# Decode attention with a GLU gate: the gate's weights moved to the front of the stream, vector-matrix products on VectorE

## The chip, the cores and the metric

The kernel runs on one core of one Trainium2 chip. A core has five engines that run side by side, each with its own list of instructions: TensorE (PE: matmul, with its weight loads as PEld), VectorE (DVE), ScalarE (ACT), GpSimd (POOL) and SyncE (SP). They meet through semaphores. Sixteen DMA engines move data between the chip's memory (HBM) and the core's own memory (SBUF, 128 partitions); here SP issues nearly all transfers, ACT a few small ones. Matmuls write to PSUM. The metric is the time of one execution in device microseconds, as the median of several runs; the profile is of one more execution, taken by the hardware profiler.

## The reference

One token is decoded. Its row x has 512 values. It is normalised, attends with 32 heads over 8192 cached keys and values of 128 each, and the result is multiplied by a gate that a GLU block computes from the same normalised row.

```python
xn = _layernorm(x, axis=-1)                                   # (1, 1, 512)
# attention: q of 32 heads of 128, caches of (1, 32, 8192, 128)
q = (xn @ wq).reshape(B, Sq, H, Dh).transpose(0, 2, 1, 3)     # wq (512, 4096)
scores = jnp.einsum("bhqd,bhkd->bhqk", q, k_cache) * (Dh ** -0.5)
p = _softmax(scores, axis=-1)
o = jnp.einsum("bhqk,bhkd->bhqd", p, v_cache)
s = o.transpose(0, 2, 1, 3).reshape(B, Sq, H * Dh) @ wo       # wo (4096, 512)
# gate
g = jnp.einsum("bsd,df->bsf", xn, w_gate)                     # (512, 1376)
u = jnp.einsum("bsd,df->bsf", xn, w_up)                       # (512, 1376)
g = _silu(jnp.einsum("bsf,fd->bsd", _sigmoid(g) * u, w_down)) # (1376, 512)
return x + s * g
```

All of it is float32. The caches are 134 MB each, wq and wo 8.4 MB each, the gate's three matrices 2.8 MB each: 293.7 MB are read once.

## The kernel before, in words

The 32 heads are taken in 16 pairs. The keys of a pair (8.39 MB) fill one *slot*: 128 partitions of 64 KB. Partitions 0 to 63 hold the first head, 64 to 127 the second, and each partition holds 128 consecutive positions of 128 values. There are three slots: `slots[0]` and `slots[1]` take the keys in turn, `slots[2]` takes the values, and before them wq.

**The queries.** wq is loaded first (`ld_wq`), then the keys of pairs 0 and 1. x comes on ACT's queue, once as a column over the partitions (`x_col`) and once as four rows (`x_row`, for the end). VectorE, TensorE and ACT compute mean and variance; `xn` is the normalised column. TensorE multiplies xn with wq: 32 matmuls with one column of xn as weights (L206), whose results lie in single rows of PSUM. ACT copies these rows (L211), TensorE spreads each over all partitions with a column of ones (L218), and ACT copies the heads to their halves of `q_all` (L225).

**One pair.** VectorE multiplies the keys in place by the query (`scores`, L281), sums each position (L282) and takes the partition's maximum (L284). TensorE transposes the maxima (L246), VectorE takes each head's maximum (L276), TensorE spreads it (L248), and ACT turns the scores into powers (`powers_of`, L294 and L296). TensorE multiplies powers and values in 32 matmuls (L255, the function `pair`) into `po`, ACT copies `po` (`parts`, L301), four small matmuls add up its pieces (L260), and VectorE divides by the sum of the powers (`heads_out`, L288 and L289). The two heads are then rows of a small tile `on`, and two DMAs on ACT's queue put them into `o_all` in the layout that the last product wants (`place`).

**What sets the order.** Everything is written out by hand. Each engine runs its list in order, and every step counts up its engine's semaphore. TensorE's 15 first pairs are a loop of its own (L265) around the same block; the last pair is written out behind it. SP issues the loads: the keys of pair i when the scores of pair i - 2 are summed, the values of pair i - 1 when the values of pair i - 2 have been used. Whatever SP has issued waits in its DMA queue, in order.

**The end.** The last values go into the slot of keys 14 (L331). Behind them come the gate's weights w_gate, w_up and w_down, into `slots[2]` as soon as values 14 are used, and then wo in six pieces of 14, 10, 4, 2, 1 and 1 rows per partition (`W_ENDS`), into the slot of keys 15. After the last pair TensorE computes the gate's two products with xn (L356), ACT and VectorE form `sg` and `hg`, VectorE transposes them in blocks (L366), TensorE multiplies with w_down (L384), and ACT and VectorE finish the gate in `g_row`. Then come wo's matmuls (L402 and L406; the results of the first 28 rows per partition are copied by ACT and folded in, L371 and L377), two VectorE operations (L416 and L418) and the output.

## Time and profile before

| what | us |
|---|---|
| median of 3 runs (lowest, highest) | 687.7 (687.37, 688.03) |
| profiled execution: its span | 685.6 |
| VectorE busy in it | 574.0 (84%) |
| TensorE busy in it | 222.1 (32%) |
| ACT busy in it | 40.9 (6%) |
| granted TensorE clock, mean | 0.664 of full speed |
| idle time of VectorE before the keys' products (L281), waiting for keys | 38.8 |

The span goes from the profiled execution's first instruction to its last; no other time is shown for that execution, so its own time is the span, and the runs' median stands 2.1 us above it. Busy shares say how long an engine had work, not that it set the end. Rows of groups read: line, engine, operation, output<-input with shapes, count | busy us, mean ns of one | idle us before it and what ended the idle time. Rows of the timeline read: start, duration, engine, line, operation, with the idle time before it and its releaser in brackets. Rows of waits read: who <- whom: total us, times, longest.

### The profile page before, as it was taken

Reading aid. Unit: us, or ns where it says so; the run is one execution under the profiler, and the core shown is the slowest. Engines: PE = TensorE matmul, PEld = TensorE weight load, DVE = VectorE, ACT = ScalarE, POOL = GpSimd, SP = SyncE. Lnnn points to the kernel's source line nnn. Section 1 sums busy time; section 2 is a strip of 40 time slices with the busy share of each in tenths; the row PEclk is TensorE's granted clock in tenths of the full one; section 3 lists DMA queues with packets and bytes.
Section 4 is the critical chain, followed back from the end, with each engine's and each line's share of the span. In section 5 each row is a group of like instructions: output and inputs, shape, how many; then the busy total and the mean of one; then the engine's idle time right before and its main releaser. Section 6 shows DMA issues by size and latency. Waiting matters only on the chain.

```text
span 685.6 us, 3694 instructions
## 1 busy us (share of the span) xinstructions
PE 222.1 (32%) x1570; PEld 62.7 (9%) x1570; DVE 574.0 (84%) x136; ACT 40.9 (6%) x122; POOL 0.7 (0%) x6
## 2 busy tenths in 40 slices
PE   0550230605041140505042140506042140605656
PEld 0110000101010010101001010101000010101121
DVE  0159999999999999989898989989898989989220
ACT  0040100000000000000001010000001010000010
POOL 0000000000000000000000000000000000000000
PEclk9965575757566575757557575756657575756798
DMA  9999999999999999999999999999999999999996
GB/s 375 440 445 451 428 428 428 432 428 428 428 436 444 448 440 428 428 428 436 428 428 428 440 444 451 428 432 428 432 432 428 428 440 436 451 436 428 405 434 285
DMA packets 6614, 293.84 MB, mean 429 GB/s; under 512 B 1096, under 2 KB 1104, under 8 KB 1616
## 3 DMA queue, kind: packets, MB, share of 16 engines
q1 hardware_dynamic: 6200, 293.74, 99.1%
q10 hardware_dynamic: 408, 0.02, 0.0%
q8 instruction: 4, 0.07, 0.0%
q14 instruction: 2, 0.02, 0.0%
HBM read 293.74 MB, written 0.00 MB: 428 GB/s over the span
## 4 chain that ended last, share of the span: by engine, by line
DMA 37%; DVE 30%; PE 0%; SPq 0%; issue 0%
DMA slot<-in_A_k_cache_dram 31%; DVE slot L281 15%; DVE sc L282 15%; DMA slot<-in_A_wo_dram 6%; PE acc L406 0%; SPq L131 0%; PE pt L246 0%; PE acc L377 0%; DVE g_row L416 0%; DVE g_row L418 0%; DVE mx L276 0%
## 5 line engine op out<-in xcount | busy, mean ns | idle before, releaser
L281 DVE TENSOR_TENSOR slot<-slot,q_all 128x16384 f32<-128x16384 f32 x16 | 275.5, 17217 | 38.8 <-DMA slot<-in_A_k_cache_dram 38.8
L282 DVE TENSOR_REDUCE sc<-slot 128x128 f32<-128x16384 f32 x16 | 275.5, 17220 | 0.6
L255 PE MATMUL po<-slot,weights 128*8 128x512 f32 x1024 | 146.7, 737 | 232.1 <-PEq L242 231.5
L255 PEld LDWEIGHTS po<-slot,weights 128*8 128x8 f32 x1024 | 30.3, 103 | 335.3 <-issue 334.6
L246 PE MATMUL pt<-ident,mx 128*1 128x128 f32 x32 | 8.8, 374 | 148.6 <-PEq L242 148.6
L301 ACT COPY o<-po 128x512 f32<-128x512 f32 x16 | 9.4, 586 | 385.2 <-PE po L255 385.2
L260 PE MATMUL pn<-o,pick 128*2 128x128 f32 x128 | 16.5, 272 | 12.8 <-PEq L242 12.8
L180 DVE TENSOR_REDUCE st<-x_col 128x1 f32<-128x4 f32 x1 | 0.2, 157 | 20.7 <-DMA x_col<-in_A_x_dram 20.7
L246 PEld LDWEIGHTS pt<-ident,mx 128*1 128x1 f32 x32 | 1.8, 80 | 154.1 <-issue 154.1
L288 DVE RECIPROCAL rl<-pn 2x1 f32<-2x1 f32 x16 | 2.3, 146 | 14.6 <-PE pn L260 14.6
L294 ACT ACTIVATE nb<-pm 128x2 f32<-128x2 f32 x16 | 2.8, 173 | 190.4 <-PE pm L248 190.4
L416 DVE TENSOR_TENSOR g_row<-g_row,acc 128x128 f32<-128x128 f32 x1 | 0.3, 289 | 15.3 <-PE acc L406 15.3
L296 ACT ACTIVATE weights<-sc,nb 64x128 f32<-64x128 f32 x32 | 12.8, 399 | 0.9
L260 PEld LDWEIGHTS pn<-o,pick 128*2 128x2 f32 x128 | 9.9, 84 | 29.6 <-issue 27.2
L248 PE MATMUL pm<-mx,ones 1*128 1x2 f32 x32 | 8.8, 344 | 7.4 <-PEq L242 7.4
L402 PE MATMUL big<-slot,o_all 128*1 128x512 f32 x56 | 9.4, 765 | 4.8 <-DMA slot<-in_A_wo_dram 4.8
L250 PE MATMUL pn<-rs,half 128*2 128x1 f32 x32 | 3.0, 163 | 23.5 <-PEq L242 23.5
L218 PE MATMUL big<-q_all,ones 1*128 1x512 f32 x16 | 8.8, 850 | 1.6 <-ACT q_all L225 0.8
L206 PE MATMUL big<-slot,xn 128*1 128x512 f32 x64 | 9.0, 726 | 0.8 <-DVE xn L198 0.8
L248 PEld LDWEIGHTS pm<-mx,ones 1*128 1x128 f32 x32 | 7.9, 306 | 14.4 <-issue 14.4
L276 DVE TENSOR_REDUCE mx<-pt 1x2 f32<-1x128 f32 x16 | 4.5, 278 | 5.2 <-PE pt L246 5.0
L182 PE MATMUL pt<-st,ones 128*128 128x1 f32 x2 | 0.6, 362 | 23.4 <-DVE st L180 23.4
(61 smaller groups left out, 62.1 us busy)
## 6 DMA issues: line engine op xcount, KB each, us to landing
slot<-in_A_wo_dram SPq DMA_DIRECT2D x1, 3584.0 KB, 32.5
slot<-in_B_w_gate_dram SPq DMA_DIRECT2D x1, 2752.0 KB, 16.8
slot<-in_B_w_up_dram SPq DMA_DIRECT2D x1, 2752.0 KB, 22.8
slot<-in_B_w_down_dram SPq DMA_DIRECT2D x1, 2560.0 KB, 27.3
slot<-in_A_wo_dram SPq DMA_DIRECT2D x1, 2560.0 KB, 38.2
slot<-in_A_wo_dram SPq DMA_DIRECT2D x1, 1024.0 KB, 40.2
o_all<-on ACTq DMA_DIRECT2D x32, 0.5 KB
slot<-in_A_wo_dram SPq DMA_DIRECT2D x1, 512.0 KB, 40.9
```

Source lines behind the costliest of these rows:

```text
L206: ins = PE.matmul(big[b][g * GP:g * GP + 1, :], xn[:, k:k + 1], wq_t[:, k, c:c + QT], start=(k == 0), stop=(k == KT - 1))
L218: spreads[t] = pe(PE.matmul(big[t % 2], ones[g * GP:g * GP + 1, :], q_row[g * GP:g * GP + 1, b, :], start=True, stop=True))
L246: PE.matmul(pt[0:1, :], mx[:, 0:1], ident, start=True, stop=True).then_inc(turned, 1)
L248: PE.matmul(pm, ones[:1, :], mx[:1, 1:3], start=True, stop=True).then_inc(spread_m, 1)
L255: ins = PE.matmul(po[g * GP:g * GP + 2 * HT, :], weights[:, j // HT, :], v[:, j * Dh:(j + HT) * Dh], start=(j < HT * NG), stop=(j >= NB - ...
L260: ins = PE.matmul(pn[:, :Dh], pick[:, b:2 * HT:HT], o1[:, b * Dh:(b + 1) * Dh], start=(b == 0), stop=(b == HT - 1))
L276: DVE.reduce_max(mx[:1, 1:3], pt[0:1, :].rearrange("o (e p) -> o e p", e=2), axis=AX.X).then_inc(reduced, 1)
L281: wait(DVE, dve(DVE.tensor_mul(k, k, qb[:, i:i + 1, :].to_broadcast([P, NB, Dh]))))
L282: summed[i] = dve(DVE.reduce_sum(sc[i % 2], k, axis=AX.X))
L296: ACT.activation(weights[h, :, e * HT:(e + 1) * HT], sc[i % 2][h].rearrange("p (g b) -> p g b", b=HT), AF.Exp, bias=nb[h, e:e + 1], scale= ...
L301: ACT.copy(o1, po).then_inc(copied, 1)
L402: ins = PE.matmul(big[0][g:g + 1, :], o_all[:, r:r + 1], wo_t[:, r, :], start=(r < NG), stop=(r + NG >= W_FOLD))
```

## The change

1. **Order of loads.** wq is loaded in two halves, and w_gate and w_up come right behind it, into `slots[0]`; then keys 0, into `slots[1]`. w_down follows into `slots[2]` once the queries are summed, keys 1 into `slots[0]` once the gate's first products are summed, values 0 into `slots[2]` once the gate is summed. Keys use the slots the other way round. Of w_down's last rows only the missing 96 are loaded, not 128. At the end the last keys and the last values are loaded in halves, and wo follows the values directly.
2. **Products on VectorE.** wq, w_gate and w_up are multiplied by xn in place on VectorE: one pass with a product (`tensor_scalar`), then three with product and sum (`scalar_tensor_tensor`). TensorE only adds up the partitions with a block of ones, which for the queries also spreads them. The 32 matmuls L206, ACT's copies L211 and the gate's 56 matmuls L356 go.
3. **x.** Only the four rows are loaded; VectorE transposes them into the column.
4. **Heads.** VectorE transposes each pair's heads into a PSUM tile `o_t`, and after the last pair four transposes put them all into `o_all`. ACT's 32 small DMAs go.
5. **TensorE's text.** TensorE's instructions are noted first (`Later`) and written out at the end: a loop of two turns, whose first turn skips the work and only jumps over it. The whole body is a block with a branch back at its end that is never taken; ACT, VectorE and TensorE carry a branch hint for it, TensorE's in front of the last pair.

SP's list from the start of the program to the first issue that waits for scores. Before:

```order
L131 DMA slot<-in_A_wq_dram 128x16384
L131 DMA slot<-in_A_k_cache_dram 128x16384 x2
L161 DMA slot<-in_A_v_cache_dram 128x16384 [waits s_pe]
L131 UNCONDITIONAL_BRANCH
L131 DMA slot<-in_A_k_cache_dram 128x16384 [waits s_dve]
```

Now:

```order
L163 DMA slot<-in_A_wq_dram 128x8192 x2
L163 DMA slot<-in_B_w_gate_dram 128x5504
L163 DMA slot<-in_B_w_up_dram 128x5504
L163 DMA slot<-in_A_k_cache_dram 128x16384
L212 UNCONDITIONAL_BRANCH
L163 DMA slot<-in_B_w_down_dram 128x5120 [waits s_pe]
L163 DMA slot<-in_B_w_down_dram 96x512
L163 DMA slot<-in_A_k_cache_dram 128x16384 [waits s_pe]
L205 DMA slot<-in_A_v_cache_dram 128x16384 [waits s_pe]
L163 DMA slot<-in_A_k_cache_dram 128x16384 [waits s_dve]
```

Four loads now stand ahead of keys 0, and w_down, keys 1 and values 0 each wait for TensorE (s_pe), where keys 1 waited for nothing.

VectorE's list between the normalisation and the first scores. Before:

```order
L198 TENSOR_SCALAR xn<-xc,st 128x4 [waits s_dve]
L228 MEMSET acc 128x128
L229 MEMSET po 128x512
L230 MEMSET weights 128x256
L231 MEMSET half 128x2
L234 MEMSET half 64x1 [waits s_dve,s_pool]
L234 MEMSET half 64x1
L236 COPY pick<-ident 32x8 x4
L131 UNCONDITIONAL_BRANCH
L281 TENSOR_TENSOR slot<-slot,q_all 128x16384 [waits s_act,s_k0]
```

Now (s_wq0 and s_wq2 are wq's halves, s_wg and s_wu the gate's matrices):

```order
L260 TENSOR_SCALAR xn<-xc,st 128x4 [waits s_dve]
L266 TENSOR_SCALAR slot<-slot,xn 128x4096 [waits s_wq0,s_dve]
L267 SCALAR_TENSOR_TENSOR slot<-slot,xn 128x4096 [waits s_dve,s_wq0]
L267 SCALAR_TENSOR_TENSOR slot<-slot,xn 128x4096 [waits s_dve,s_wq2]
L267 SCALAR_TENSOR_TENSOR slot<-slot,xn 128x512 [waits s_dve]
L267 SCALAR_TENSOR_TENSOR slot<-slot,xn 128x512 x7
L266 TENSOR_SCALAR slot<-slot,xn 128x1376 [waits s_wg]
L267 SCALAR_TENSOR_TENSOR slot<-slot,xn 128x1376 [waits s_dve] x3
L266 TENSOR_SCALAR slot<-slot,xn 128x1376 [waits s_wu,s_dve]
L267 SCALAR_TENSOR_TENSOR slot<-slot,xn 128x1376 [waits s_dve] x3
L315 MEMSET big 128x512 [waits s_pe,s_act,s_dve]
L316 TENSOR_TENSOR slot<-slot,big 128x352
```

Nineteen passes over weights stand ahead of the first scores, the gate's behind the queries'.

SP's list from the last values on. Before:

```order
L331 DMA slot<-in_A_v_cache_dram 128x16384 [waits s_dve]
L131 DMA slot<-in_B_w_gate_dram 128x5504 [waits s_valued]
L131 DMA slot<-in_B_w_up_dram 128x5504
L131 DMA slot<-in_B_w_down_dram 128x5120
L131 DMA q_all<-in_B_w_down_dram 128x512
L131 DMA slot<-in_A_wo_dram 128x7168 [waits s_dve]
```

Now:

```order
L430 DMA slot<-in_A_v_cache_dram 128x8192 [waits s_dve]
L430 DMA slot<-in_A_v_cache_dram 128x8192
L163 DMA slot<-in_A_wo_dram 128x7168 [waits s_dve]
L163 DMA slot<-in_A_wo_dram 128x5120
L163 DMA slot<-in_A_wo_dram 128x2048
```

The gate's four loads no longer stand between the last values and wo.

The diff, cut to its core:

```diff
-    ld_wq = load(SP, "wq", wq_t, wq.rearrange("(p k) c -> p k c", k=KT))
+    wq_v = wq.rearrange("(p k) c -> p k c", k=KT)
+    ld_wq = [load(SP, f"wq{n}", wq_t[:, n:n + 2, :], wq_v[:, n:n + 2, :]) for n in (0, 2)]
+    wg_t, wu_t = (slots[0][:, n * KT * F:(n + 1) * KT * F].rearrange("p (k f) -> p k f", f=F) for n in range(2))
+    ld_g = load(SP, "wg", wg_t, w_gate.rearrange("(p k) f -> p k f", k=KT))
+    ld_u = load(SP, "wu", wu_t, w_up.rearrange("(p k) f -> p k f", k=KT))
...
     load_keys(0)
-    load_keys(1)
-    ld_x = load(ACT, "x", x_col, xv.rearrange("(p k) -> p k", k=KT))
+    once = nc.alloc_registers("once")
+    nc.regs_mov(once, 0)
+    nc.br("body")
+    body = ctx.enter_context(ExitStack())
+    body.enter_context(nc.body("body"))
+    hints = {e: e.mark_branch_hint_location() for e in (ACT, DVE)}
...
+    def in_place(w, k, cols=slice(None)):
+        y = w[:, 0, cols]
+        if k == 0:
+            return dve(DVE.tensor_scalar(y, y, xn[:, 0:1], None, op0=ALU.mult))
+        return dve(DVE.scalar_tensor_tensor(y, w[:, k, cols], xn[:, k:k + 1], y, op0=ALU.mult, op1=ALU.add))
...
+    for t in range(NQ):
+        c = slice(t * QT, (t + 1) * QT)
+        wait(PE, in_place(wq_t, KT - 1, c), copies.get(t - 2))
+        spreads[t] = pe(PE.matmul(big[t % 2], ones, wq_t[:, 0, c], start=True, stop=True))
...
+    load(SP, "wd", wd_t, w_down[:FP * P, :].rearrange("(p r) e -> p r e", r=FP), spreads[NQ - 1])
+    ld_d = load(SP, "wd", wd_last[:FL, :], w_down[F - FL:, :])
...
+    load_keys(1, rows[1])
...
+    gated = column_sums(big[1], s_gate)
+    load_values(0, gated)
...
     def heads_out(i):
...
-        outs[i] = dve(DVE.tensor_scalar(on[i % 2][:2], pn[:, :Dh], rl[:2], None, op0=ALU.mult))
+        wait(DVE, dve(DVE.tensor_scalar(on[:2], pn[:, :Dh], rl[:2], None, op0=ALU.mult)))
+        o = o_t[:WR, 2 * WP * i:2 * WP * i + Dh].rearrange("r (e a) -> r a e", a=WP)
+        turned_out[i] = dve(DVE.transpose(o, on[:WR].rearrange("e (a r) -> e a r", r=WR)))
...
+    with nc.Fori(0, 2, engines=pe_only) as visit:
+        with PE.engine.If(visit > 0):
+            PE.play(before)
+            with nc.Fori(0, NP - 1, engines=pe_only):
+                PE.play(each)
+    hints[PE.engine] = PE.engine.mark_branch_hint_location()
+    PE.play(last)
+    PE.play(after)
...
+    nc.regs_alu(once, once, 1, op=ALU.add)
+    for e in (ACT, DVE, PE.engine, POOL, SP):
+        br = e.br_lt(once, 1, on_true="body", on_false="done")
+        if e in hints:
+            br.branch_hint(hints[e])
```

In the new text `before` is TensorE's work up to the first pair, `each` one pair of the loop, `last` the last pair and `after` wo's matmuls.

## The prediction

> **What bounds the kernel now.** I read the page's first three parts first, then the chain of work that ended last, then the waits, and last the two ends of the run as a timeline and in narrow windows.

> ```profile
> span 685.6 us, 3694 instructions
> ...
> DMA  9999999999999999999999999999999999999996
> ...
> q1 hardware_dynamic: 6200, 293.74, 99.1%
> q10 hardware_dynamic: 408, 0.02, 0.0%
> q8 instruction: 4, 0.07, 0.0%
> q14 instruction: 2, 0.02, 0.0%
> HBM read 293.74 MB, written 0.00 MB: 428 GB/s over the span
> ```

> The DMA line is 9 in every slice but the last, and SP's queue (q1) alone holds the sixteen DMA engines for 99.1% of the span. The chain names VectorE for 30%, which can mislead; its pieces in order of time say why:

> ```profile
> 526.40 17.24 DVE slot L281
> ...
> 560.91 42.81 DMA slot<-in_A_k_cache_dram
> ...
> 603.74 17.24 DVE slot L281
> ...
> 639.57 40.94 DMA slot<-in_A_wo_dram
> ...
> 681.82 0.44 PE acc L406 x8
> 682.26 0.02 issue
> 682.28 0.30 DVE g_row L416
> ...
> 682.61 0.29 DVE g_row L418
> ```

> VectorE starts a keys' product only when the keys land. Between 526.40 and 603.74 four tiles of 8.39 MB passed: 19.34 us each, 434 GB/s. Keys land 42.8 us after their issue, though one tile takes 19.3: each transfer stands behind a whole one already queued. So the queue is never empty, and VectorE's work only decides when the next issue comes, not when its bytes do. At 434 GB/s, 293.74 MB take 677 us; with some 2 us until the first bytes and 3.9 us after the last landing (681.8, the last matmuls' start, to 685.6) hardly 3 us are left to gain anywhere.

> Where those 3 us lie, windows at the end show (columns: stretch, its length, busy time of the engines, TensorE's granted clock, DMA share, GB/s):

> ```profile
> 670.00:675.00 5.00, 4.09 (x20) 0.73 (x24) 0.00 (x0) 0.00 (x0) 0.00 (x0) 0.50 0.99 426
> ...
> 679.00:680.00 1.00, 1.00 (x12) 0.19 (x8) 0.00 (x0) 0.00 (x0) 0.00 (x0) 1.00 0.96 377
> 680.00:681.00 1.00, 0.93 (x22) 0.31 (x16) 0.00 (x0) 0.48 (x1) 0.00 (x0) 1.00 0.38 145
> 681.00:682.00 1.00, 0.96 (x32) 0.42 (x24) 0.00 (x0) 0.10 (x1) 0.00 (x0) 1.00 0.13 43
> ```

> The mean DMA engine stops at 680 + 0.38 + 0.13 = 680.5, the last landing comes at 681.8: the sixteen end unevenly, and that costs 1.3 us.

> **The change, part by part.** *The stream's order and length.* Since the sum of bytes decides, moving the gate's 8.2 MB from the end to the start is worth nothing by itself. The bytes fall by 32 rows of 2 KB (64 KB, 0.15 us at 428 GB/s). Halving wq, the last keys and the last values gives shorter rows; the wo pieces, with rows still shorter, moved 426 GB/s from 670 to 675 (row above), so I cost it at nothing, with 0.3 us as the other end.

> *Is the queue still fed at the start?* This is the cover for all that VectorE now does, and it has to be counted out.

> ```profile
> 0.96 0.39 SPq L131 DMA_DIRECT2D slot<-in_A_wq_dram  x1
> 23.14 0.16 DVE L180 TENSOR_REDUCE st<-x_col 128x1 f32<-128x4 f32 x1 [20.65 <-DMA x_col<-in_A_x_dram]
> 25.97 0.23 DVE L198 TENSOR_SCALAR xn<-xc,st 128x4 f32<-128x4 f32 x1
> ...
> slot<-in_A_wq_dram SPq DMA_DIRECT2D x1, 22.0
> x_col<-in_A_x_dram ACTq DMA_DIRECT2D x1, 2.0 KB, 22.1
> ...
> L281 DVE TENSOR_TENSOR slot<-slot,q_all 128x16384 f32<-128x16384 f32 x16 | 275.5, 17217 | 38.8 <-DMA slot<-in_A_k_cache_dram 38.8
> L218 PE MATMUL big<-q_all,ones 1*128 1x512 f32 x16 | 8.8, 850 | 1.6 <-ACT q_all L225 0.8
> L225 ACT COPY q_all<-big 64x256 f32<-64x256 f32 x16 | 5.9, 367 | 5.5 <-PE big L218 5.2
> ```

> From wq's landing at 0.96 + 22.0 = 23.0 and 19.34 us per 8.39 MB, the new queue lands wg (2.82 MB, 6.5 us) at 29.5, wu at 36.0, keys 0 at 55.3, wd at 61.8, keys 1 at 81.1, values 0 at 100.5. The same row of VectorE gives 1.051 ns per element. Half of wq lands at 23.0 - 9.7 = 13.3. x was 22.1 us on the way in 128 pieces, 8 for each engine, 2.8 us a turn between wq's pieces; as four pieces it needs one or two turns, say 6 us, and its mean and variance took 3.1 us (23.14 to 26.20). So x is ready at 13.3; if it were not, the end lies 15 us of slack away. The passes over wq: two of 4096 (4.3 us each) to 21.9, the third after 23.0 to 27.3, the last in eight pieces of 0.6 to 32.1. TensorE's sum (0.85) and ACT's two copies (0.73) beside each piece keep near that pace, so the eighth sum is done by 34. Then wd can be issued, 21 us before keys 0 end. The gate's eight passes of 1376 (1.45 us) are done at 43.7, since they follow the queries' passes, and TensorE's sums at 45: keys 1 are issued 16 us before the queue would run dry at 60.8 (1 us from an issue to first bytes). Values 0 wait for the gate's last sum:

> ```profile
> 662.46 2.31 PE L384 MATMUL big<-slot,o 128*1 128x512 f32 x18 [2.68 <-DVE o L367]
> 666.37 0.28 ACT L390 ACTIVATE g_row<-big 128x128 f32<-128x128 f32 x1 [0.52 <-PE big L377]
> ```

> that stretch took 3.9 us before, so 61.8 + 4 = 66, or 70 at half the clock, against 80. Keys 2 wait for the first scores, 55.3 + 34.5 = 89.8 against 99.5. All are fed; the work taken from TensorE and ACT was beside the stream too. Cost: 0.

> *Each pair.* A stream transpose is added on VectorE and two small DMAs of the ACT queue go. VectorE waits 38.8 us over ten products (row above), some 3 us a pair late in the run; a transpose is 0.2 us (row below). Cost: 0.

> *The end.* wo now follows the last values directly, so what follows the values has 19.3 us of wo as cover instead of that and the gate's 19.5.

> ```profile
> 642.44 9.84 PE L255 MATMUL po<-slot,weights 128*8 128x512 f32 x64 [0.57 <-DMA slot<-in_A_v_cache_dram]
> 652.35 0.59 ACT L301 COPY o<-po 128x512 f32<-128x512 f32 x1 [10.82 <-PE po L255]
> 654.34 0.34 DVE L289 TENSOR_SCALAR on<-pn,rl 2x128 f32<-2x128 f32 x1
> 670.91 5.81 PE L402 MATMUL big<-slot,o_all 128*1 128x512 f32 x28 [4.61 <-DMA slot<-in_A_wo_dram]
> 676.87 3.60 PE L402 MATMUL big<-slot,o_all 128*1 128x512 f32 x28 [0.15 <-DMA slot<-in_A_wo_dram]
> ...
> L366 DVE STREAM_TRANSPOSE o<-q_all 128x32 f32<-128x32 f32 x10 | 1.3, 197 | 0.0
> ...
> 660.00:665.00 5.00, 2.54 (x22) 0.54 (x22) 2.26 (x13) 0.00 (x0) 0.00 (x0) 1.00 1.09 461
> 665.00:670.00 5.00, 0.60 (x11) 0.10 (x8) 0.77 (x2) 0.86 (x2) 0.00 (x0) 0.86 0.96 413
> ```

> Let E be the last landing. The second half of the values lands at E - 19.3; half its matmuls, 32, take 4.1 us at full clock (3.60 / 28 each) or 6.6 at half (5.81 / 28). From there to the scaled heads it took 652.28 to 654.68, 2.4 us, and five transposes add 1.2: the heads stand placed at E - 11.6 or E - 9.1. wo's first 14 rows land at E - 10.8. At full clock TensorE then follows the landings. At half clock throughout the first 14 rows end at E - 3.3, the next ten (full clock by then, 2.6) at E - 0.7, four more at E + 0.3, copy and fold at E + 1.3: 1.2 us late. The clock was 1.00 after the 2.7 us gap before L384 and 0.50 (670 to 675, row further up) after the 4.6 us gap before L402; the gaps here are about 2.7, nearest the first. Cost: 0, other end +1.2.

> *Unevenness.* The code and small packets fall on single DMA engines: the four code packets of q8 (16 KB each, 0.6 us at one engine's sixteenth of 428 GB/s), which I take for TensorE's, the longest text, two more of q14, and 408 packets of the ACT queue. The new program has 165 matmuls in TensorE's text instead of 239, no x_col, no head placements; its early visit fetches once more. Bounds: all 1.3 us gained, or 0.6 lost if one more packet falls on the last engine. No view says which engine a packet takes; I take half the gain, -0.6.

> Sum: 685.6 - 0.15 - 0.6 = 684.9 for the profiled execution. The runs' median stands 2.1 us above its span, which I carry over: **687.0 us**, for this case 686.3 to 688.3.

> **The rivals.** *All evenness gained (faster).* If no code packet falls in the stream, E moves to the mean engine's 680.5, less 0.15, and the vanished small packets another 0.1: 686.1 us. For it speaks the shorter text, against it that the two ends of TensorE's code still have to come.

> *TensorE meets missing code at the end (slower).* The program now loops twice over blocks and jumps. If the block behind the last pair is not there when TensorE reaches wo, its fetch queues behind the stream: one turn was 2.8 us for x_col. After the landing of wo's second piece, at E - 4.8, TensorE has no such slack, so it shows in full from there: 687.0 + 2.8 = 689.8. Against it: in the trace of before no matmul group at the end waits for code. [...]

> *The two-tensor product runs at half speed (slower).* Then 3 x 4096 + 6 x 1376 = 20544 elements cost 21.6 us more: the queries' passes end at 43.9, the gate's at 64.1, keys 1 are issued at 65.1 against 60.8, and the queue is empty for 4.3 us: 691.3. It decides as soon as the passes grow by 16 us; if the one-tensor passes run at double speed, 3.6 us come back. The row that is nearest, L281, reads two f32 tensors at 1.051 ns, the same as the one-tensor sum, and speaks against it. [...]

> **How the numbers follow.** 0.2% of 687.7, 1.4 us, is about what a measurement of this kernel tells from no change. Chances: forecast 0.55, evenness 0.17, missing code 0.15, half speed 0.13. Faster is the second case, 0.17. Slower is the third, most of the fourth (0.10) and the cold clock's tail of the first (0.02): 0.27. The rest, 0.56, is the same. The range goes from just under the second case, 685.9, to 690.0, just over the third; it leaves out most of the fourth and the tails, under 0.2.

> **What would show it.** Right: DMA 9 from the first slice to the last; no wait of keys 1 or values 0 beyond their turn; the product passes at 4.3 and 1.45 us; wo's matmuls waiting for wo's landings; the last landing at 681.1, with a steeper fall of the DMA share. Wrong: passes of 8.6 us and a dip in the DMA line near 60 us; an idle TensorE inside wo's rows with all landed; more q8 packets than four.

## The result and the profile after

The changed kernel takes 690.04 us (median of five, 689.67 to 691.09), the kernel before, run beside it, 687.37 us (687.30 to 688.03). The ratio is 1.0038, with a 95% interval of 1.0027 to 1.0049: 2.6 us slower. The forecast was 687.0, no change. One execution of the run e3 below (765.71 us) fell into a slower state of the chip, and the ratios leave it out.

The span did not grow. These are the top and the DMA part of the page of the changed kernel:

```profile
span 685.7 us, 3402 instructions
...
DMA  8999999999999999999999999999999999999996
...
q1 hardware_dynamic: 6600, 293.67, 99.1%
q8 instruction: 2, 0.03, 0.0%
q10 hardware_dynamic: 8, 0.00, 0.0%
HBM read 293.67 MB, written 0.00 MB: 428 GB/s over the span
```

685.7 us against 685.6, the same 428 GB/s, the same 99.1% of the DMA engines' time for SP's queue. The small packets of ACT's queue (q10) have gone from 408 to 8, and q8 has two code packets inside the span instead of four. The end of the chain of waits, in order of time (start, duration, what):

```profile
657.68 24.18 DMA slot<-in_A_wo_dram
681.91 0.44 PE acc L37 x8
682.38 0.30 DVE g_row L471
682.70 0.29 DVE g_row L473
```

The last landing comes at 681.9, as before, and what follows it is what followed it before. (L37 is the line that plays TensorE's noted instructions; it stands for all of them.) Narrow windows of the changed kernel, the last of them behind the span (stretch, its length, busy time of the engines, TensorE's clock, DMA share, GB/s):

```profile
679.00:680.00 1.00, 1.00 (x12) 0.19 (x8) 0.00 (x0) 0.00 (x0) 0.00 (x0) 1.00 0.91 352
680.00:681.00 1.00, 0.93 (x22) 0.31 (x16) 0.00 (x0) 0.43 (x1) 0.00 (x0) 1.00 0.07 27
681.00:682.00 1.00, 0.92 (x28) 0.41 (x24) 0.00 (x0) 0.16 (x1) 0.00 (x0) 1.00 0.03 12
685.70:690.00 4.30, 0.00 (x0) 0.00 (x0) 0.00 (x0) 0.00 (x0) 0.00 (x0) 0.50 0.01 2
```

And the window behind the span of the kernel before:

```profile
685.60:690.00 4.40, 0.00 (x0) 0.00 (x0) 0.00 (x0) 0.00 (x0) 0.00 (x0) 0.78 0.00 0
```

Two things are to be read. First, the profiled execution took 690.04 us, 4.3 us more than its span, and the four others stand 4.2 to 5.5 us above theirs. The kernel before was timed 96 times beside the experiments, each time with its own span: it stands 1.7 to 1.9 us above it, 1.8 in the middle. (The 2.1 us named ahead of the change is the median of three runs less the span of one execution, and is 0.3 us too much.) So some 2.5 of the 2.7 us between the medians lie behind the last instruction that the span counts. There the DMA engines did nothing before (share 0.00, 0 GB/s) and do something now (0.01, 2 GB/s). The packets of the trace say what: one code packet of 16 KB on q8 at 685.05 us, which begins 0.6 us ahead of the span's end and ends behind it, and one of 8 KB on q14 at 687.71. A stretch with no busy engine is shown by no group, wait or chain of the profile; only the windows and the difference between time and span give it away. Second, the mean DMA engine now stops at 680 + 0.07 + 0.03 = 680.1, earlier than before (680.5), but the last one still at 681.9.

### The profile page after: what moved, and what is told of

The parts are those of the page before. It is cut to its first block, busy times and chain, and to the rows that moved or that the text cites. A ratio compares the mean times of both kernels' runs of the same rounds, so it can differ in the third digit from the quotient of the medians.

```text
span 685.7 us, 3402 instructions
## 1 busy us (share of the span) xinstructions
PE 211.8 (31%) x1422; PEld 74.8 (11%) x1422; DVE 606.2 (88%) x166; ACT 39.9 (6%) x120; POOL 0.7 (0%) x6
## 3 DMA queue, kind: packets, MB, share of 16 engines
q1 hardware_dynamic: 6600, 293.67, 99.1%
## 4 chain that ended last, share of the span: by engine, by line
DVE 51%; DMA 35%; SPq 0%; issue 0%; PE 0%
DMA slot<-in_A_k_cache_dram 31%; DVE sc L381 25%; DVE slot L380 25%; DMA slot<-in_A_wo_dram 4%; SPq L163 0%; DVE on L388 0%; DVE o_t L390 0%; DVE mx L372 0%; DVE mx L383 0%; PE pt L37 0%; PE acc L37 0%; DVE g_row L471 0%; DVE g_row L473 0%; DVE rl L387 0%; DVE g_row L417 0%
## 5 line engine op out<-in xcount | busy, mean ns | idle before, releaser
L380 DVE TENSOR_TENSOR slot<-slot,q_all 128x16384 f32<-128x16384 f32 (+1 forms) x17 | 275.6, 16214 | 34.0 <-DMA slot<-in_A_k_cache_dram 34.0
L381 DVE TENSOR_REDUCE sc<-slot 128x128 f32<-128x16384 f32 (+1 forms) x17 | 275.7, 16216 | 0.6
L37 PE MATMUL po<-slot,weights 128*8 128x512 f32 x1024 | 146.8, 729 | 263.9 <-PEq L37 263.9
L37 PEld LDWEIGHTS po<-slot,weights 128*8 128x8 f32 x1024 | 45.5, 102 | 351.9 <-issue 345.1
L37 PE MATMUL pt<-ident,mx 128*1 128x128 f32 x32 | 8.6, 367 | 107.8 <-PEq L37 107.8
L402 ACT COPY o<-po 128x512 f32<-128x512 f32 x16 | 9.4, 587 | 416.9 <-PE po L37 416.9
L267 DVE SCALAR_TENSOR_TENSOR slot<-slot,xn 128x512 f32<-128x512 f32 (+2 forms) x16 | 24.3, 1554 | 3.0 <-DMA slot<-in_A_wq_dram 2.7
L37 PE MATMUL pn<-o,pick 128*2 128x128 f32 x128 | 16.5, 272 | 12.8 <-PEq L37 12.8
L37 PE MATMUL big<-slot,ones 128*128 128x512 f32 (+3 forms) x52 | 12.2, 496 | 25.5 <-DVE slot L267 23.6
L37 PEld LDWEIGHTS pt<-ident,mx 128*1 128x1 f32 x32 | 1.8, 80 | 112.0 <-issue 112.0
L37 PEld LDWEIGHTS pn<-o,pick 128*2 128x2 f32 x128 | 9.9, 84 | 29.5 <-issue 27.1
L37 PE MATMUL pm<-mx,ones 1*128 1x2 f32 x32 | 8.6, 337 | 7.8 <-PEq L37 7.8
L37 PE MATMUL pn<-rs,half 128*2 128x1 f32 x32 | 3.0, 163 | 23.7 <-PEq L37 23.7
L37 PE MATMUL big<-slot,o_all 128*1 128x512 f32 x56 | 8.9, 725 | 2.8 <-DMA slot<-in_A_wo_dram 2.8
L37 PE MATMUL big<-slot,o 128*1 128x512 f32 (+1 forms) x22 | 4.5, 934 | 16.3 <-DMA slot<-in_B_w_down_dram 16.3
L37 PEld LDWEIGHTS pm<-mx,ones 1*128 1x128 f32 x32 | 7.7, 298 | 14.6 <-issue 14.6
L37 PEld LDWEIGHTS big<-slot,ones 128*1 128x1 f32 (+1 forms) x52 | 4.0, 133 | 34.2 <-DVE slot L267 28.3
L283 ACT COPY q_all<-big 64x256 f32<-64x256 f32 x16 | 5.9, 368 | 23.1 <-PE big L37 22.6
```

The lines of the kernel that those rows point to most:

```text
L37: ins = getattr(self.engine, name)(*args, **kwargs)
L267: return dve(DVE.scalar_tensor_tensor(y, w[:, k, cols], xn[:, k:k + 1], y, op0=ALU.mult, op1=ALU.add))
L283: copies[t] = act(ACT.copy(qb[h, 2 * t:2 * t + 2, :], q[h, :, e, :]))
L380: wait(DVE, dve(DVE.tensor_mul(k[:, j, :], k[:, j, :], qb[:, i:i + 1, :].to_broadcast([P, n, Dh]))))
L381: summed[i] = dve(DVE.reduce_sum(sc[i % 2][:, j], k[:, j, :], axis=AX.X))
L402: ACT.copy(o1, po).then_inc(copied, 1)
```

## The experiments

Each run was timed beside the kernel before, whose median was 687.46, 687.57, 687.40 and 687.56 us in the four groups of runs (e1 to e4, e5 to e8, e9 to e12, e13 to e16). A hint here is the pair of calls `mark_branch_hint_location` and `branch_hint`, which ties a place in an engine's list to the branch at the end of the body; that branch is never taken. The length of VectorE's list counts all its instructions in the compiled program, jumps included. Times are medians; the code packets are those of the one profiled execution, by their start; in these traces one of q8 has 16 KB, one of q14 8 KB.

| run | hints on | VectorE's list, instructions | us | ratio (95%) | code packets on q8; q14, us |
|---|---|---|---|---|---|
| changed kernel | ACT, VectorE, TensorE | 200 | 690.04 | 1.0038 (1.0027 to 1.0049) | 6.7, 685.1; 687.7 |
| e1 | none | 199 | 687.58 | 1.0003 (0.9994 to 1.0012) | 6.5, 665.9; 60.5, 170.0 |
| e2 | ACT, TensorE | 199 | 690.11 | 1.0033 (1.0021 to 1.0045) | 6.3, 687.1; 59.9, 687.6 |
| e3 (no visit) | all | 196 | 689.96 | 1.0036 (1.0023 to 1.0049) | 105.0, 688.0; 687.9 |
| e4 (no visit, no branch) | none | 190 | 687.60 | 1.0002 (0.9993 to 1.0010) | 107.5, 667.1; 59.5, 192.1 |
| e5 (kernel before) | ACT, VectorE | 191 | 687.55 | 1.0000 (0.9991 to 1.0009) | 48.9, 647.7, 661.0, 682.4; none |
| e6 | TensorE | 199 | 689.88 | 1.0035 (1.0022 to 1.0048) | 6.6, 688.0; 60.6, 170.2, 687.9 |
| e7 | ACT, VectorE | 200 | 689.80 | 1.0033 (1.0022 to 1.0045) | 6.4, 665.7; 687.5 |
| e8 (visit ahead of the stream) | TensorE | 199 | 690.69 | 1.0035 (1.0021 to 1.0048) | 2.4, 687.7; 60.8, 168.4, 688.1 |
| e9 | ACT | 199 | 687.51 | 1.0000 (0.9991 to 1.0009) | 6.5, 665.9; 60.7, 687.9 |
| e10 | VectorE | 200 | 690.39 | 1.0039 (1.0025 to 1.0053) | 6.4, 665.7; 170.0, 687.5, 690.1 |
| e11 (list shortened) | ACT, VectorE | 190 | 687.51 | 1.0001 (0.9992 to 1.0010) | 6.4, 665.9; none |
| e12 (kernel before, list longer) | ACT, VectorE | 206 | 688.87 | 1.0020 (1.0011 to 1.0029) | 49.3, 647.4, 661.4, 681.7; 683.9, 686.3 |
| e13 | TensorE, late | 199 | 687.60 | 1.0002 (0.9993 to 1.0011) | 6.6, 666.8; 60.6, 170.0 |
| e14 | VectorE, late | 200 | 687.67 | 1.0001 (0.9992 to 1.0010) | 6.4, 665.8; 60.7, 170.0, 687.8 |
| e15 (kernel before, list longer) | ACT, VectorE | 200 | 689.75 | 1.0034 (1.0022 to 1.0046) | 51.5, 647.1, 660.0, 681.4; 686.6, 689.1 |
| e16 | all, late | 200 | 687.62 | 1.0006 (0.9997 to 1.0015) | 6.7, 666.8; 60.7, 170.0 |

### Which part of the change costs the time

The first theory was that the hints, and not the moved work, put missing code behind the end. Rivals were the early visit of TensorE's blocks, the branch and jump, and the new way of placing heads. e1 takes away the hints and nothing else:

```
-    hints = {e: e.mark_branch_hint_location() for e in (ACT, DVE)}
+    hints = {}
...
-    hints[PE.engine] = PE.engine.mark_branch_hint_location()
```

> The changed kernel without any branch hint; the never-taken branch and the two-turn loop stay. Theory A (the 2.7 us lie behind the last instruction: the hints keep the code that follows from being fetched ahead, so it is fetched on demand after the span): time 687.4, about 1.8 us above the span, and the page's queue list shows instruction packets of q14 inside the span again. Rival B (the branch and the extra block at the end cost the time, whatever the hints): 690.0, still 4.3 above the span.

687.58 us: all of the loss is gone. Behind the span of e1:

```profile
685.70:690.00 4.30, 0.00 (x0) 0.00 (x0) 0.00 (x0) 0.00 (x0) 0.00 (x0) 0.77 0.00 0
```

The DMA engines are idle there again. e2 takes the hint from VectorE alone:

```
-    hints = {e: e.mark_branch_hint_location() for e in (ACT, DVE)}
+    hints = {e: e.mark_branch_hint_location() for e in (ACT,)}
```

> The changed kernel without VectorE's hint alone; ACT's and TensorE's stay. Theory A1 (it is VectorE's code that is missing at the end; its text is the longer of the two that fetch by q14): 687.4, one q14 packet inside the span. Theory A2 (TensorE's or ACT's code is what is missing): 690.0. Rival B: 690.0.

690.11 us, where theory A1 had 687.4: VectorE's hint isn't needed for the loss. The loss isn't the same each time: of the six executions of e2 the fastest took 688.00 us. e3 leaves the hints and takes the loop of two turns away, so that TensorE's code is met for the first time when it is needed:

```
-    with nc.Fori(0, 2, engines=pe_only) as visit:
-        with PE.engine.If(visit > 0):
-            PE.play(before)
-            with nc.Fori(0, NP - 1, engines=pe_only):
-                PE.play(each)
+    PE.play(before)
+    with nc.Fori(0, NP - 1, engines=pe_only):
+        PE.play(each)
```

> The changed kernel without the loop of two turns around TensorE's blocks; hints and branch stay. Theory C (one DMA engine ends 1.4 us after the others because the early visit fetches a code packet at 6.7 us): the code packet comes later or not at all, the last landing comes by up to 1.4 us earlier unless a later packet falls on a late engine: span 684.3 to 685.7. Rival D (the late engine comes from the first loads themselves): span 685.7, unchanged. On the time behind the span theory A says 4.3 us as before, 688.6 to 690.0 in all; if the visit were the cause of it, 687.4 or less.

689.96 us: the visit has no part in the loss. Its trace tells something else, on the unevenness. Of the sixteen completions of each load, the first and the last of wq's first half were 1.9 us apart in the changed kernel, 15 of them within 0.4 us; and to the end one completion stays that late (1.8 us at the last wo piece). The only code packet so early is that of TensorE at 6.67 us. Without the visit they lie within 0.41 us, and those of the load that landed last ahead of the packet at 105 us within 0.36; those of the next load are 1.92 us apart, and without the late one 0.34. So one code packet into the running stream made one DMA engine late, and in this run the stream didn't give the time back: the last wo piece's completions are still 1.91 us apart. The theory's landing 1.4 us earlier didn't come, because the later packet did the same as the early one. The windows at the end of e3:

```profile
679.00:680.00 1.00, 1.00 (x12) 0.19 (x8) 0.00 (x0) 0.00 (x0) 0.00 (x0) 1.00 0.81 309
680.00:681.00 1.00, 0.94 (x22) 0.31 (x16) 0.00 (x0) 0.44 (x1) 0.00 (x0) 1.00 0.06 25
681.00:682.00 1.00, 0.91 (x28) 0.41 (x24) 0.00 (x0) 0.14 (x1) 0.00 (x0) 1.00 0.03 12
```

One engine alone fills the last two windows (a sixteenth is 0.06), with or without the visit. e4 leaves out the hints, the branch and the visit:

```
-    once = nc.alloc_registers("once")
...
-    hints = {e: e.mark_branch_hint_location() for e in (ACT, DVE)}
...
-        br = e.br_lt(once, 1, on_true="body", on_false="done")
```

> The changed kernel with neither hints nor the never-taken branch nor the loop of two turns: the moved gate, VectorE's products and the transposes alone. Theory A: 1.8 us above its span, which is 684.3 to 685.7 after theory C and 685.7 after rival D: 686.1 to 687.5. If the cost were in the moved work itself (neither A nor B): 690.

687.60 us. What is left of the change, the moved gate, the products on VectorE, the transposes and the halved loads, is worth nothing either way: 1.0002 (0.9993 to 1.0010).

### Do hints cost by themselves?

If any hint costs, then the kernel before must lose with one too. e5 puts the branch and the hints on ACT and VectorE into it; e6 and e7 split the hints of the changed kernel between TensorE and the other two.

```
     (e5, in the kernel before)
+    once = nc.alloc_registers("once")
+    nc.regs_mov(once, 0)
+    nc.br("body")
...
+    hints = {e: e.mark_branch_hint_location() for e in (ACT, DVE)}
...
+    for e in (ACT, DVE, PE, POOL, SP):
+        br = e.br_lt(once, 1, on_true="body", on_false="done")
+        if e in hints:
+            br.branch_hint(hints[e])
```

> The kernel before, unchanged in its work, with one part of the change alone: the never-taken branch at the end and a hint for it on ACT and VectorE. Theory A (these hints keep the code behind the end from being fetched ahead): the two q14 packets vanish from the span, at least one comes after it, and the time is 690.0, 2.5 above the kernel before with a span of 685.6. Rival E (the cost belongs to the new arrangement of work, which the hints only uncover): 687.4.

A miss: 687.55 us, no loss. Both q14 packets of the kernel before (193.7 and 225.5 us) are gone, and none comes behind the end. So the hints did act, and it cost nothing (687.55 against 687.57 us).

```
     (e6)
-    hints = {e: e.mark_branch_hint_location() for e in (ACT, DVE)}
+    hints = {}
     (e7)
-    hints[PE.engine] = PE.engine.mark_branch_hint_location()
```

> The changed kernel with TensorE's hint alone. Theory A with ACT or VectorE as the culprit (their packets came at 687.6 and 687.7 in the runs that cost time): q14 packets inside the span, one q8 packet behind it, 687.4. If TensorE's packet behind the end costs as much: 690.0.

> The changed kernel with the hints of ACT and VectorE alone. Theory A with ACT or VectorE as the culprit: 690.0. With TensorE as the culprit: 687.4. On the unevenness (theory C): two q8 packets inside the span and a late engine as in the changed kernel, span 685.6.

689.88 and 689.80 us: TensorE's hint alone is enough, and so are the other two. They don't add up: with all three the changed kernel took 690.04 us. What the engines do behind the end stands in no trace. Behind the span of e6:

```profile
685.70:690.00 4.30, 0.00 (x0) 0.00 (x0) 0.00 (x0) 0.00 (x0) 0.00 (x0) 0.50 0.02 6
```

6 GB/s here against 0 in e1: the packet of q8 that came at 665.9 us without the hint comes at 688.0 with it. e8 keeps TensorE's hint and lets SP's first load wait until the visit's first turn is through, so that the early packet falls ahead of the stream:

```
+    seen = semaphore("s_seen")
+    SP.wait_ge(seen, 1)
...
     with nc.Fori(0, 2, engines=pe_only) as visit:
...
+        PE.engine.nop().then_inc(seen, 1)
```

> The changed kernel with TensorE's hint alone, and SP issues its first load only after TensorE's first turn over its blocks. Theory C: TensorE's code packet then passes ahead of the stream, no engine is late (0.4 us between the engines instead of 1.9), and the last landing comes 1.4 us earlier, less the delay of the first load of some 0.5: span 684.8, time 686.6 if TensorE's hint is free, 689 if not. Rival D (the lateness does not come from the code packet): span 686.2.

690.69 us. The packet came at 2.4 us, ahead of the stream, and the completions of the first load lay 0.8 us apart instead of 1.9. But the stream began 0.9 us later (first packets at 2.85 instead of 1.97 us), at the end they were 1.1 us apart, and the last landing was at 682.1 instead of 681.9. Theory C had 0.4 us between the engines and a span of 684.8; with 685.9 that is a miss. What evenness gave (0.7 us), the later start took (0.9). Two of its six executions took only 688.36 and 688.69 us, so the price of TensorE's hint, too, differs from one execution to the next.

### The length of the list

e5 forced a new theory. VectorE's list has 191 instructions in e5 and 200 in the changed kernel. If a hint stops the fetch of the engine's next block of code, then that costs only where the list runs on into this block. e9 and e10 set the hint on ACT alone (a shorter list than in the kernel before) and on VectorE alone:

```
     (e9; e10 has DVE instead of ACT)
-    hints = {e: e.mark_branch_hint_location() for e in (ACT, DVE)}
+    hints = {e: e.mark_branch_hint_location() for e in (ACT,)}
...
-    hints[PE.engine] = PE.engine.mark_branch_hint_location()
```

> The changed kernel with the hint on ACT alone (VectorE's and TensorE's are left out). Length theory: a hint stops the fetch of the engine's next block of code, and that costs only where the engine's list runs on into that block. ACT's list of the new kernel is shorter than in the old one, where its hint cost nothing, so 687.5 us and no code packet behind the last instruction. Rival, any hint costs in the new program because its body is reached by a jump: 689.9 us, with a code packet behind the end.

> The changed kernel with the hint on VectorE alone. Length theory: VectorE's list is 9 instructions longer than in the old kernel with hints and runs into a block that was not fetched: 689.9 us, with one packet of q14 behind the end. Rival, any hint costs: 689.9 us too. If it takes 687.5 us, then VectorE's is not the one, and ACT's must be.

687.51 and 690.39 us, as the length theory has it for both. Two details missed. In e10 two packets of q14 come behind the end and not one, and in e9 one comes at 687.9 us where none was expected. That packet isn't shown to be free: the profiled execution in which it stands took 688.21 us, 2.5 us above its span, and the ten others of e9 stand 1.8 to 1.9 us above theirs. The median hides it. The same is seen wherever the list has 199 or 200 instructions and no early hint costs the large price: of the 55 executions of e1, e9, e13, e14 and e16 ten stand 2.3 to 3.5 us above their span. Of the 33 of e4, e5 and e11, with 190 or 191 instructions, none stands more than 2.1 us above it. What makes the difference in these ten was not tested.

The two runs also say whose the early q14 packets are: ACT's hint removes the one at 170.0 us, VectorE's the one at 60.7. Both come more than 500 us ahead of the span's end (685.5 and 685.7 us).

e11 and e12 change the length alone. e11 is the changed kernel with hints on ACT and VectorE, with ten instructions less on VectorE:

```
-    c_eps = dve(DVE.memset(eps_t, EPS))
+    c_eps = pool(POOL.memset(eps_t, EPS))
+    pool(POOL.memset(weights, 0.0))
+    pool(POOL.memset(on, 0.0))
...
-    dve(DVE.memset(weights, 0.0))
-    dve(DVE.memset(on, 0.0))
...
-        wait(PE, in_place(wq_t, KT - 1, c), copies.get(t - 2))
+        if t == 0:
+            last_pass = in_place(wq_t, KT - 1)
+        wait(PE, last_pass, copies.get(t - 2))
...
-    hints[PE.engine] = PE.engine.mark_branch_hint_location()
```

> The changed kernel with the hints on ACT and VectorE, and VectorE's list 10 instructions shorter: wq's last pass in one piece instead of eight, three clears moved to GpSimd. The same work, the gate still in front. Length theory: VectorE's list fits again as in the old kernel, so 687.5 us and no code packet behind the end. Rival, any hint costs in the new program: 689.9 us. The longer last pass delays the queries by some 4 us, beside slack of 13 us, so it costs nothing in either.

687.51 us against the 689.80 of e7: ten instructions in the first 40 us of the program decide on 2.3 us behind its end. The DMA part of its page:

```profile
q1 hardware_dynamic: 6600, 293.67, 99.1%
q8 instruction: 2, 0.03, 0.0%
q10 hardware_dynamic: 8, 0.00, 0.0%
```

And its window behind the span:

```profile
685.70:690.00 4.30, 0.00 (x0) 0.00 (x0) 0.00 (x0) 0.00 (x0) 0.00 (x0) 0.77 0.00 0
```

No q14 row, and 0 GB/s behind the span: in this execution no packet of q14 comes inside the span or behind it, and the time is that of the kernel before (687.51 against 687.40 us). e12 is the kernel before with the hints of e5 and fifteen instructions more on VectorE:

```
-    dve(DVE.memset(acc, 0.0))
+    for n in range(16):
+        dve(DVE.memset(acc[:, n * GC // 16:(n + 1) * GC // 16], 0.0))
```

> The kernel before with the branch and the hints on ACT and VectorE, and VectorE's list 15 instructions longer: one clear is split into sixteen. Length theory: VectorE's list now runs past the block as in the new kernel, so 689.9 us with a packet of q14 behind the end, where the same kernel without the fifteen took 687.55. Rival, it is the new program's jumps or order that make a hint costly: 687.5 us.

688.87 us: slower than e5, so the old kernel can be made to lose in the same way, but by 1.3 us and not 2.4. The end of its timeline (start, duration, engine, line):

```profile
682.79 0.29 DVE L425 TENSOR_TENSOR g_row<-g_row,x_row 128x128 f32<-128x128 f32 x1
683.11 0.63 SPq L429 DMA_DIRECT2D out_dram<-g_row  x1
```

And the window behind it:

```profile
683.00:685.00 2.00, 0.00 (x0) 0.00 (x0) 0.08 (x1) 0.00 (x0) 0.00 (x0) 0.99 0.02 5
```

A code packet of q14 begins at 683.9 us, within 1 us of the end of VectorE's last addition (683.08). The loss now lies inside the span, and there the trace shows who waits. Each engine closes its list with a DRAIN (line L67, in the sequencer's queue, so it counts as busy in no view). Two rows of `--source L67` of e12 (operation, count, duration in ns, first and last start in us):

```profile
L67 ACTq DRAIN  x1: 8/8/8, 684.1 to 684.1; - x1
L67 DVEq DRAIN  x1: 117/117/117, 685.7 to 685.7; - x1
```

And VectorE's row of e15, a run of the next section whose list is six instructions shorter:

```profile
L67 DVEq DRAIN  x1: 10/10/10, 684.0 to 684.0; - x1
```

In e12 the four other engines drain between 684.13 and 684.17 us, VectorE only at 685.69: 1.5 us later than the others, 1.8 us after the start of that packet. SP's wait for the output takes 0.03 us there and 0.37 in e15, so 0.3 us of the 1.5 are hidden beside the output's write, and 1.2 remain; the medians say 1.3. The spans say it too: 686.6 to 687.3 us in the runs of e12, against 685.4 to 686.2 in those of e5.

### Where the hint stands, and where the list crosses

Two points were open: whether a hint stops the fetch ahead or sends the end of the list to the wrong place wherever it stands, and why e12 lost less. e13 sets TensorE's hint behind its last matmul, e14 VectorE's behind the last pair, e16 all three so late; e15 is e12 with a list of the changed kernel's length.

```
     (e13; hints = {} at the start)
-    hints[PE.engine] = PE.engine.mark_branch_hint_location()
     PE.play(last)
     PE.play(after)
+    hints[PE.engine] = PE.engine.mark_branch_hint_location()
     (e14; no hint at the start and none on TensorE)
     heads_out(NP - 1)
+    hints = {e: e.mark_branch_hint_location() for e in (DVE,)}
     (e15, in e12)
-    for n in range(16):
+    for n in range(10):
```

> The changed kernel with a hint on TensorE alone, set behind its last matmul and not ahead of the last pair. If a hint stops the fetch ahead: at that place the last block of code has long been asked for, so 687.5 us, and the packet of q8 near 666 us is back. If a hint costs wherever it stands because the branch is taken for one that jumps: 689.9 us, with a packet of q8 behind the end.

> The changed kernel with a hint on VectorE alone, set behind the last pair and not at the start. If a hint stops the fetch ahead: 687.5 us, and a packet of q14 near 60 us that was missing with the hint at the start. If it costs wherever it stands: 690.4 us as with the hint at the start, with packets of q14 behind the end.

> The kernel before with the branch and the hints on ACT and VectorE, and VectorE's list 9 instructions longer, just as long as in the changed kernel (15 longer in the run ahead of this, which took 688.87 us). If the cost goes by where the list crosses into the missing block: 689.9 to 690.4 us, and the packet of q14 behind the span instead of at 683.9 us. If the old kernel simply loses less: 688.9 us again.

> The changed kernel with all three hints, each set near the end of its engine's list. If a hint stops the fetch ahead, the whole change without its cost: 687.5 us. If hints cost wherever they stand: 689.9 us.

687.60, 687.67, 689.75 and 687.62 us: all four as the theory of the stopped fetch has them. With late hints the packets at 60.7 and 170.0 (q14) and 666.8 us (q8) are back. e10 and e14 differ only in the place of VectorE's hint; the q14 row of the page of e10, then of e14:

```profile
q14 instruction: 1, 0.01, 0.0%
```

```profile
q14 instruction: 2, 0.02, 0.0%
```

One packet less inside the span, and 2.7 us more in the median. The span of e15 is 685.6 us; its windows from the output's write on:

```profile
683.00:685.00 2.00, 0.00 (x0) 0.00 (x0) 0.00 (x0) 0.00 (x0) 0.00 (x0) 0.76 0.00 1
685.00:687.00 2.00, 0.00 (x0) 0.00 (x0) 0.00 (x0) 0.00 (x0) 0.00 (x0) 0.50 0.02 4
687.00:691.00 4.00, 0.00 (x0) 0.00 (x0) 0.00 (x0) 0.00 (x0) 0.00 (x0) 0.62 0.01 2
```

Against e12 the traffic has moved behind the span: six instructions less, and the first q14 packet behind the last addition begins at 686.6 instead of 683.9 us, 1.0 us behind the span's end. The loss is 2.2 us (689.75 against 687.55). Without hints code packets come while the engines still work, and the median shows no cost (e1: 60.5, 170.0 and 665.9 us, ratio 1.0003); with VectorE's hint ahead of it the packet at 60.5 is missing, and two come behind the end (e10: 687.5 and 690.1 us, ratio 1.0039).

Four things stay open. Whose the q14 packet at 687.8 to 688.1 us in e6, e8, e9 and e14 is, and why it comes in some executions, can't be read from the trace. Whether a hint stops the fetch or turns it to a block that is already there can't be told either; in both cases the packet is missing. That TensorE's hint acts through the place of its code was shown by its place (e13), not by the length of its list: a kernel with TensorE's list shortened was not tried. And a kernel that beats both was not found: the change without its cost (e16, e1, e4) stands level with the kernel before.

## Why the prediction was wrong, point by point

The forecast was 684.9 for the profiled execution and 2.1 behind its span; measured were 685.7 and 4.3. Of the 3.0 us that were missing, 2.2 lie behind the span and 0.8 in it. Had the distance of the kernel before been taken from executions with their own spans, 1.8 us, it would have been 2.5 and 0.8.

**The step that failed: "The runs' median stands 2.1 us above its span, which I carry over."** The change touches just what lies there. It adds hints to three engines, and two of them cost the time by themselves: TensorE's 2.3 us (e6, 689.88 against the 687.58 of e1) and VectorE's 2.8 (e10, 690.39). Without the hints (e1), with late hints (e13 and e16) and with a shorter list (e11), most executions stand 1.8 to 2.0 us above their span again, as the kernel before does. The sum had no term for the hints at all.

**The second step: half of the unevenness gained, -0.6, and -0.15 for fewer bytes.** The mean DMA engine did stop 0.4 us earlier, but the last landing didn't move, 681.9 against 681.8: the early visit's own code packet puts one engine 1.9 us behind from the first 15 us on (the completions of wq's first half; e3). The bound "0.6 lost if one more packet falls on the last engine" had the mechanism; the estimate of 0.6 us for 16 KB was too small, a packet cost 1.6 us of lateness (1.92 less 0.36 in e3).

**The queue at the start: right.** Steps in the timeline of the changed kernel:

```profile
8.24 0.40 DVE L241 STREAM_TRANSPOSE g_row<-x_row 128x128 f32<-128x128 f32 x1 [4.42 <-DMA x_row<-in_A_x_dram]
...
14.67 2.35 DVE L266 TENSOR_SCALAR slot<-slot,xn 128x4096 f32<-128x4096 f32 x1 [2.94 <-DMA slot<-in_A_wq_dram]
...
39.53 0.80 SPq L163 DMA_DIRECT2D slot<-in_B_w_down_dram  x2
...
47.58 0.34 SPq L163 DMA_DIRECT2D slot<-in_A_k_cache_dram  x1
...
56.64 17.22 DVE L380 TENSOR_TENSOR slot<-slot,q_all 128x16384 f32<-128x16384 f32 x1 [7.04 <-DMA slot<-in_A_k_cache_dram]
63.87 4.49 PE L37 MATMUL big<-slot,o 128*1 128x512 f32 x22 [16.34 <-DMA slot<-in_B_w_down_dram]
...
69.52 0.33 SPq L205 DMA_DIRECT2D slot<-in_A_v_cache_dram  x1
```

x is there at 8.2 (6 forecast) and waits 2.9 us for wq, so nothing hangs on it. wd is issued at 39.5 (34 forecast) and keys 1 at 47.6 (45), while VectorE takes up keys 0 at 56.6 and TensorE wd at 63.9, each as it lands; values 0 follow at 69.5 (66 to 70). The queue always had work.

**The half-speed rival: fell.** By the groups with shapes kept apart:

```profile
L267 DVE SCALAR_TENSOR_TENSOR slot<-slot,xn 128x1376 f32<-128x1376 f32 x6 | 9.9, 1652 | 0.2
L267 DVE SCALAR_TENSOR_TENSOR slot<-slot,xn 128x4096 f32<-128x4096 f32 x2 | 9.0, 4484 | 2.8 <-DMA slot<-in_A_wq_dram 2.7
L267 DVE SCALAR_TENSOR_TENSOR slot<-slot,xn 128x512 f32<-128x512 f32 x8 | 5.4, 748 | 0.0
L390 DVE STREAM_TRANSPOSE o_t<-on 32x128 f32<-32x128 f32 x16 | 5.0, 315 | 0.5
L266 DVE TENSOR_SCALAR slot<-slot,xn 128x4096 f32<-128x4096 f32 x1 | 2.4, 2353 | 2.9 <-DMA slot<-in_A_wq_dram 2.9
```

The two-tensor pass takes 4.48 us for 4096 elements (4.3 forecast; 8.6 by the rival), the one-tensor pass only 2.35, about half; the forecast had 4.3 for both. The gate's two-tensor passes take 1.65 us (1.45 forecast). The two-tensor pass over wq runs at about half the rate of the one-tensor pass, 1.09 us for 1000 elements against 0.57, but that is near the rate of the keys' product (1.05), which reads two tensors itself and which the rival had halved. No pass shows the rival's 2.1 us for 1000 elements (8.6 for 4096): at 1376 elements it was 1.20, at 512 1.46.

**Each pair: right.** A transpose takes 0.3 us, and VectorE still waits for keys:

```profile
L380 DVE TENSOR_TENSOR slot<-slot,q_all 128x16384 f32<-128x16384 f32 x15 | 258.3, 17219 | 34.0 <-DMA slot<-in_A_k_cache_dram 34.0
```

**The end: right.** TensorE begins wo when its first piece lands, 0.3 us after the last of the four transposes into `o_all`, and waits for the landing of the second piece too:

```profile
669.75 0.92 DVE L425 STREAM_TRANSPOSE o_all<-o_t 32x32 f32<-32x32 f32 x4
670.96 5.30 PE L37 MATMUL big<-slot,o_all 128*1 128x512 f32 x28 [2.15 <-DMA slot<-in_A_wo_dram]
676.92 3.60 PE L37 MATMUL big<-slot,o_all 128*1 128x512 f32 x28 [0.67 <-DMA slot<-in_A_wo_dram]
```

The heads stand at 670.7, 11.2 us before the last landing (11.6 or 9.1 forecast), and cost nothing.

**The rivals.** "All evenness gained" fell with the late engine. "TensorE meets missing code at the end", 689.8 us, came nearest to the time, and its kind was right: code packets that come late, 2.8 us by the forecast, 2.2 to 2.8 measured. Its place and cause were wrong: not inside wo's rows, where the changed kernel shows no such gap, but behind the last instruction; not by the loop of two turns (e3), but by the hints; and VectorE's list as much as TensorE's. That the price agrees is luck: the 2.8 us were x_col's turn behind a full stream (an estimate, 22.1 us over eight pieces), and here the packets come when the stream has ended (687.7 us, the last landing at 681.9).

## What to carry to other kernels

Compare an execution's time with its own span before anything is carried over: what lies between them is a cost of its own, and here hints (1.8 to 2.5 us in e1, 4.2 to 5.5 in the changed kernel) and list lengths (4.2 to 4.7 in e7, 1.8 to 2.0 in e11) moved it, with spans of 685.4 to 686.0 us in all four. A branch hint isn't free advice: set near the start of the list or ahead of the last pair it cost this kernel 2.5 us (690.04 against the 687.58 of e1), so set it near the end of the list (e16, 687.62 us) or leave it out, and compare the program with all hints removed. Where one saturated stream set the time, work moved beside it was worth nothing (e4, 687.60 against 687.46 us), and one code packet into it made one DMA engine 1.6 us late (e3), ten times the 0.15 us forecast for the shorter stream. Read all executions and not the median alone, above all the profiled one: e9's packet looked free only because the median came from other executions.
